# A routed mixture of experts on one core: chunks of 512 tokens instead of 256, gathers ahead of scatters that keep no order, one DMA for each expert's matrix

## The chip, the core and the metric

The kernel runs on one core of a Trainium2 chip. The core has a tensor engine (PE, whose weight loads the profile lists as PEld), a vector engine (DVE), a scalar engine (ACT), GpSimd (POOL) and a sync engine (SP) that issues DMAs. Each works through its own queue in order; they wait for one another by semaphores. [...] The metric is the device time of one execution in microseconds (us), as the median over runs.

## The reference

Three steps follow each other on an input of 8 x 3072 x 256: the real part of a two-dimensional Fourier transform, a gated network over all 24576 tokens, and a routed mixture of 8 experts. Only the last is touched by the change. With x the 24576 tokens of 256 numbers:

```python
logits = x @ w_gate                      # 24576 x 8
order = np.argsort(-logits.flatten())
# in this order a (token, expert) pair is taken if the token is still free
# and the expert has fewer than cap = 24576 // 8 = 3072 tokens
for e in range(8):
    mask = assigned == e                 # 3072 tokens
    h = np.maximum(x[mask] @ w1[e], 0.0) # 256 -> 1024
    out[mask] = h @ w2[e]                # 1024 -> 256
```

## The kernel before

The transform takes the span's first 315 us, the gated network runs to about 2016 us, the routed experts (class Moe2) fill the rest. All matrix products keep float32's precision by splitting each operand in a high and a low part (names ending in h and l) of type float32r and adding three products: high by high, high by low, low by high.

Moe2 works in eight rounds r, one expert closing in each; in round r PE computes that expert's 3072 tokens while the routing of the next expert runs beside it on DVE and ACT. The routing is a chain: a search over 32 bits for the threshold (one step per beat, with a tiny product cs, L1098 and L1100, between counts junk on DVE, L1113, and jka on ACT, L1116), then best (L1176), the ranks and the picks, which give idx, the token numbers of each slot. beat hands a share of this work to each of PE's steps, want forces it where a gather needs it.

A round has 12 chunks c of 256 tokens, a chunk has 4 steps g. What happens in a step is written out in run:

- plan holds the gathers (L1218, POOL: a DMA by index for 128 tokens, two for a chunk, into xg) and the loads of the next expert's weights (wload, L1227: w0r by two DMAs at step (10, 1), w1r by eight at step (10, 3)). wsplit makes w0h, w0l, w1h and w1l of them in quarters, at the steps of CFG['sp'].
- ffn1 is 12 matmuls with 256 moving columns (L1277 to L1279) into one PSUM tile; ACT makes hh of it (L1282), DVE hl (L1283).
- ffn2 of the step two back (lag 2) is 12 matmuls with 256 columns (L1297 to L1299). After a chunk's last, ACT copies the two accumulators to y (L1302) and POOL scatters each to out by the token numbers in tok (L1303).
- For the next chunk xsplit makes gh on ACT and gl on DVE at step 1 (L1254, L1255), and xprep turns them on PE at steps 2 and 3, four float32r transposes against identr each (L1265), with an ACT copy to xh or xl behind (L1266).

All scatters write the tensor out, so each waits until the one ahead has landed. Queues keep the order in which run writes the instructions; POOL's holds gathers, weight loads, scatters and the little copies tok.

The line that sets when gathers are asked for:

```python
at = (r, c - 2, 0) if c > 2 else (r - 1, *CFG[f'g{c}'])
```

with g0 = (10, 2), g1 = (10, 3), g2 = (12, 2), the last meaning step 2 of chunk 0.

Of the kernel before, what the change touches and what calls it, by code (L numbers as in the profile page):

```python
# [90 lines left out]
class Narrow:  # L91
    """weights of double precision as float32, in DRAM, a part at a time"""
# [20 lines left out]
    def clamp_one(self, i, t):  # L113
        """the magnitude's high word, within float32's exponents"""
# [18 lines left out]
    def once(self, src, dst, w, t):  # L133
        """a small part, into a tile"""
# [16 lines left out]
def fft_phase(tc, x, xm, c_odd, c_even, c_dim, c_alt, PQ_d, R_d, narrow=(), nxt=None):  # L151
    nc = tc.nc
# [13 lines left out]
    # rows 384 + 768 i of every batch  # L166
# [293 lines left out]
    # the first batch  # L460
# [47 lines left out]
    # the last batch, with the next phase's preparation beside it  # L508
# [27 lines left out]
def _token_ids():  # L536
    """true token of partition p in tile T = (block, half, sign)"""
    ids = np.zeros((128, 192), np.int32)
    p = np.arange(128)
    for blk in range(48):  # L540
        for sub in range(2):
# [4 lines left out]
            plus = np.where(cls == 1, k, S - k)      # U + V  # L546
            minus = np.where(cls == 1, S - k, k)     # U - V
# [6 lines left out]
def _lay_w(wg, wv):  # L554
    """by (gate or value, half): rows 0 to 127; an empty row and rows 255 down to 129. Row 128 by (matrix, f-tile)"""
# [5 lines left out]
class Moe1:  # L561
# [12 lines left out]
    def gv_load(self, c):  # L574
        """three f-tiles of the gate and value weights, rows 0 to 127 and 256 down to 129"""
# [27 lines left out]
    def task(self, k, arg):  # L603
        """the weights' preparation beside the end of the transform"""
# [30 lines left out]
    def small(self):  # L635
# [4 lines left out]
        # (-1)^l by partition: -1 + 2 * (sum of the identity's even columns)  # L640
# [11 lines left out]
    def open_keep(self, keep):  # L652
# [9 lines left out]
        # the table with the sigmoid, which has the other functions too  # L662
# [14 lines left out]
    def wo_load(self, c):  # L677
        """two f-tiles of the output weights"""
# [11 lines left out]
    def wo_turn(self, c):  # L690
        """two f-tiles of the output weights, turned, in two parts"""
# [12 lines left out]
    def wo_gate(self, c):  # L704
        """the output weights' product with the router's, to stand behind them"""
# [32 lines left out]
    def prep(self, raw, part, pool=None):  # L738
        """row 128's share of P, and the parts of P and Q"""
# [49 lines left out]
    def mini_load(self):  # L789
        """token 1536 of every batch, for which V is zero"""  # L790
# [71 lines left out]
    def hand_over(self):  # L862
        """the routing's start"""
# [11 lines left out]
    def run(self, LAG=4):  # L875
# [73 lines left out]
CFG = {'NV': 768, 'T': (1, 1, 1, 2, 1), 'cap': 0.2, 'f1': 2, 'f2': 2, 'g0': (10, 2), 'g1': (10, 3), 'g2': (12, 2),  # L949
# [6 lines left out]
def _route_consts():  # L956
# [5 lines left out]
    # slots; an expert's weights' rows, by its number from the end, with their multipliers; the numbers from the end  # L962
    slot = q[:, None] + 128 * np.arange(24)[None]
    wb = np.concatenate([q[:, None] + 128 * np.arange(2)[None] + 256 * NE,
                         q[:, None] + 128 * np.arange(8)[None] + 1024 * NE], 1)
    wm = np.array([-256] * 2 + [-1024] * 8)[None].repeat(128, 0)
# [5 lines left out]
class Moe2:  # L972
    def __init__(self, tc, w1, w2, out, c_mats, c_io, c_num, rounds=NE):
        self.tc, self.nc = tc, tc.nc
        self.w1 = w1.rearrange("e d f -> (e d) f")
        self.w2 = w2.rearrange("e f d -> (e f) d")
# [3 lines left out]
    def open_keep(self, keep, L, ident, X2_d):  # L980
        """what routing keeps, before the last of the logits"""
# [8 lines left out]
        self.num = keep.tile([128, 52], F32, name="num")  # L990
# [9 lines left out]
    def fill_keep(self):  # L1000
# [4 lines left out]
        self.slot, self.wb, self.wm, self.rio = num[:, 0:24], num[:, 24:34], num[:, 34:44], num[:, 44:52]  # L1005
# [5 lines left out]
    def grow(self, g, i):  # L1011
        """the first round's V for 16 tiles, in three steps"""
# [10 lines left out]
    def turn(self, p, c, n):  # L1023
        """n blocks of K's columns from block c on; the last tiles stand first"""
# [6 lines left out]
    def count0(self, i, c, n, junk):  # L1031
        """how many of some of K's columns are not negative"""
# [4 lines left out]
    def odd(self, kk):  # L1037
        """the columns from CFG['NV'] on with the last bit set in the order of floats, for the sign's sum"""
# [20 lines left out]
    def route(self, r):  # L1059
        """the expert that closes in round r: its number and its tokens' ranks"""  # L1060
# [75 lines left out]
        # ranks in the order (partition, tile): those above the threshold, then those at it  # L1136
# [4 lines left out]
        # the expert's weights' rows  # L1141
        wi = R.tile([128, 10], I32, name="wi", bufs=2)
# [28 lines left out]
    def best(self, out, V, lim, op):  # L1171
        """the greatest over the experts, each under its limit or with its penalty"""
# [5 lines left out]
    def pick(self, r):  # L1178
        """idx[r], slot by slot: pick the row of ranks that holds the slot, count the tiles before it"""
# [34 lines left out]
    def gather(self, r, c):  # L1214
        x = self.R.tile([128, 2, XW], F32, name="xg", bufs=CFG['xb'])
        for t in range(2):
            j = 2 * c + t
            self.nc.gpsimd.indirect_dma_start(  # L1218
                out=x[:, t], out_offset=None, in_=self.X2_d,
                in_offset=bass.IndirectOffsetOnAxis(ap=self.idx[r][:, j:j + 1], axis=0))  # L1220
        self.xg[r, c] = x
# [244 lines left out]
```

## Time and profile before

| | |
|---|---|
| median of 3 runs | 3421.25 us (3420.2 to 3422.5) |
| span of the profiled execution | 3409.2 us |
| around the span, against the median | 12.05 us |
| PE busy | 3192.7 us, 94% |
| DVE, POOL, ACT busy | 79%, 57%, 48% |
| mean granted clock of PE | 0.970 |

The span runs from the first to the last instruction. PE is "busy" while a matmul is in flight; matmuls overlap, so how fast they go is read from the distance of their starts. In a timeline a row gives the start, the length, the engine, the line of the kernel, the operation and its tiles; a bracket gives the idle time of the engine before it and who ended it. "issue" and "remote" are idle times for which the profile shows no releaser among the core's instructions.

### The profile page before, as it was taken

What the parts mean: (1) busy time and instruction counts of PE and PEld (TensorE: products, weight loads), DVE (VectorE), ACT (ScalarE), POOL (GpSimd) and SP (SyncE); (2) the same over time, 40 slices, a digit from 0 to 9 for tenths busy, and PEclk for the clock granted to TensorE, in tenths of its full rate; (3) what the DMA queues carried; (4) which work ended last, traced back from release to release, by engine and by line L of the source; (5) the groups of instructions that cost most, each with busy time, mean ns of one, the idle gap of its engine ahead of it and who ended that gap; (6) DMA issues with size and microseconds to landing.
All of it is one profiled execution on the core that took longest, in us unless ns stands there. A gap on an engine that the chain in (4) does not pass through costs nothing.

```text
span 3409.2 us, 68465 instructions
## 1 busy us (share of the span) xinstructions
PE 3192.7 (94%) x25857; PEld 3147.1 (92%) x25857; DVE 2700.6 (79%) x5727; ACT 1630.9 (48%) x3078; POOL 1944.9 (57%) x1933
## 2 busy tenths in 40 slices
PE   6787999999999999999999973999999999999998
PEld 5776999999999999999999963999999999998998
DVE  8998788888888888888888888777877777775332
ACT  3334344445444444444444444646465555553333
POOL 4656677777777777777777742343434343433432
PEclk8999999999999999999999986999999999999999
DMA  5547011111111111111111001121212121111211
GB/s 220 174 156 209 23 27 30 36 30 36 29 36 28 37 27 30 36 30 36 30 36 29 27 14 41 42 63 42 65 42 63 43 63 51 53 53 51 60 48 37
DMA packets 105016, 185.72 MB, mean 54 GB/s; under 512 B 15885, under 2 KB 80486, under 8 KB 101614
## 3 DMA queue, kind: packets, MB, share of 16 engines
q1 hardware_dynamic: 80430, 113.35, 11.5%
q0 software_dynamic: 23808, 67.92, 6.6%
q8 instruction: 204, 3.34, 0.4%
q14 instruction: 126, 1.03, 0.1%
q10 hardware_dynamic: 448, 0.07, 0.0%
HBM read 112.74 MB, written 68.53 MB: 53 GB/s over the span
## 4 chain that ended last, share of the span: by engine, by line
PE 84%; DVE 9%; issue 4%; DMA 1%; another core or an unknown queue 1%; ACT 1%; POOL 0%; SPq 0%; POOLq 0%; ACTq 0%; DVEq 0%
PE acc L786 8%; PE acc L785 8%; PE acc L787 8%; PE uv L760 8%; PE uv L761 8%; PE uv L762 8%; PE f L1277 6%; PE f L1297 6%; PE f L1279 5%; PE f L1278 5%; PE f L1299 5%; PE f L1298 5%; PE xt L1265 2%; DVE tm L1176 1%; PE rt L1204 1%
## 5 line engine op out<-in xcount | busy, mean ns | idle before, releaser
L906 POOL TENSOR_TENSOR h<-gt,z 128x512 f32<-128x512 f32 x575 | 748.1, 1301 | 437.3 <-ACT gt L921 437.3
L908 ACT CAST hh<-h 128x512 fp32r<-128x512 f32 x576 | 358.1, 622 | 746.6 <-POOL h L906 726.7
L760 PE MATMUL uv<-pqh,gh 128*128 128x256 f32 x2304 | 651.8, 283 | 9.1 <-DVE z L775 9.1
L786 PE MATMUL acc<-ol,hh 128*128 128x264 f32 x2304 | 656.3, 285 | 0.0
L785 PE MATMUL acc<-oh,hh 128*128 128x264 f32 x2304 | 655.6, 285 | 0.0
L787 PE MATMUL acc<-oh,hl 128*128 128x264 f32 x2304 | 655.4, 284 | 0.0
L761 PE MATMUL uv<-pql,gh 128*128 128x256 f32 x2304 | 653.0, 283 | 0.0
L762 PE MATMUL uv<-pqh,gl 128*128 128x256 f32 x2304 | 649.7, 282 | 0.0
L770 DVE SCALAR_TENSOR_TENSOR us<-bc,w,uv 128x256 f32<-128x256 f32 x1152 | 501.9, 477 | 159.4 <-PE uv L762 150.0
L1303 POOL DMA_INDIRECT out_dram<-y,tok x192 | 200.1, 1042 | 702.8 <-ACT y L1302 461.2
L1283 DVE SCALAR_TENSOR_TENSOR hl<-f,hh 128x512 fp32r<-128x512 f32 x384 | 265.0, 690 | 344.6 <-ACT hh L1282 323.1
L917 POOL TENSOR_TENSOR hl<-h,hh 128x320 fp32r<-128x320 f32 x574 | 507.0, 883 | 0.0
L1297 PE MATMUL f<-w1h,hh 128*128 128x256 f32 x1536 | 450.7, 293 | 9.5 <-ACT y L1302 7.5
L1277 PE MATMUL f<-xh,w0h 128*128 128x256 f32 x1536 | 452.8, 295 | 1.8 <-issue 1.8
L760 PEld LDWEIGHTS uv<-pqh,gh 128*128 128x128 f32 x2304 | 436.2, 189 | 10.2 <-issue 9.3
L1278 PE MATMUL f<-xl,w0h 128*128 128x256 f32 x1536 | 435.5, 284 | 2.4 <-issue 2.4
L762 PEld LDWEIGHTS uv<-pqh,gl 128*128 128x128 f32 x2304 | 437.4, 190 | 0.0
L1299 PE MATMUL f<-w1h,hl 128*128 128x256 f32 x1536 | 435.4, 283 | 1.3 <-issue 1.3
L1279 PE MATMUL f<-xh,w0l 128*128 128x256 f32 x1536 | 435.9, 284 | 0.6 <-issue 0.4
L1298 PE MATMUL f<-w1l,hh 128*128 128x256 f32 x1536 | 433.8, 282 | 2.0 <-issue 2.0
L761 PEld LDWEIGHTS uv<-pql,gh 128*128 128x128 f32 x2304 | 435.2, 189 | 0.0
L785 PEld LDWEIGHTS acc<-oh,hh 128*128 128x128 f32 x2304 | 435.2, 189 | 0.0
(440 smaller groups left out, 7692.9 us busy)
## 6 DMA issues: line engine op xcount, KB each, us to landing
X_d<-x SPq DMA_DIRECT2D x48, 528.0 KB
xt<-in_x_dram SPq DMA_DIRECT2D x24, 1024.0 KB
pq<-PQ_d SPq DMA_DIRECT2D x48, 256.0 KB
bc<-R_d SPq DMA_DIRECT2D x48, 256.0 KB
PQ_d<-po SPq DMA_DIRECT2D x24, 384.0 KB
dw<-in_wgv_dram SPq DMA_DIRECT2D x16, 384.0 KB
PQ_d<-po SPq DMA_DIRECT2D x8, 386.0 KB
dw<-in_moe_w_out_dram SPq DMA_DIRECT2D x8, 384.0 KB
```

The source lines that it names most:

```text
L760: pe.matmul(o, wh, h[:, q], start=True, stop=False)
L761: pe.matmul(o, wh, l[:, q], start=False, stop=False)
L762: pe.matmul(o, wl, h[:, q], start=False, stop=True)
L785: pe.matmul(o, x, wh, start=(ft == 0), stop=False)
L786: pe.matmul(o, x, wl, start=False, stop=False)
L787: pe.matmul(o, y, wh, start=False, stop=(ft == NF - 1))
L906: (g if n < N else v).tensor_mul(h[m], gt.pop(m), z.pop(m)[:, :, 1])
L1277: pe.matmul(p[:, i], wh[:, d, s], xh[:, d], start=(d == 0), stop=False)
L1278: pe.matmul(p[:, i], wh[:, d, s], xl[:, d], start=False, stop=False)
L1279: pe.matmul(p[:, i], wl[:, d, s], xh[:, d], start=False, stop=(d == 1))
L1297: pe.matmul(o, hh[:, i, s], wh[:, f], start=(f == 0), stop=False)
L1299: pe.matmul(o, hl[:, i, s], wh[:, f], start=False, stop=(f == 7))
```

## The change

All of it is in Moe2, but for docstrings and comments that go away and for the host's layout of the weights.

- A chunk is 512 tokens, six to a round; the steps are counted as before by (c, g) with c from 0 to 11, two c to a chunk. ffn1 of a step makes 128 hidden rows for 512 tokens: 6 matmuls with 512 columns. ffn2 is 12 matmuls with 256 columns as before, for four groups of 128 tokens; two accumulators share a PSUM bank, and y holds two of them.
- xsplit and xprep give way to xturn: four float32 transposes against ident straight from xg, ACT's copy xh, and DVE's subtraction xl from the same PSUM tile xt, of which there is one. The two halves of the next chunk's columns stand at steps 2 and 3 of the odd c.
- Gathers for c > 1 are planned at (r, c - 2 - c % 2, c % 2), the first two at steps 2 and 3 of (r - 1, 10).
- The scatters are put in a group without dependences among themselves ("rows").
- w1 and w2 are laid out on the host so that a partition's share of an expert's matrix is one row of 8 KB; wload is one DMA, wi one column.
- At the start, tiles 2 and 3 are picked and gathered before the first turn.

```diff
     def wload(self, r, k):
         w = self.R.tile([128, 2, F2] if k == 0 else [128, 8, D], F32, name=f"w{k}r")
-        src, n, o = (self.w1, 2, 0) if k == 0 else (self.w2, 8, 2)
-        for i in range(n):
-            self.nc.gpsimd.indirect_dma_start(
-                out=w[:, i], out_offset=None, in_=src,
-                in_offset=bass.IndirectOffsetOnAxis(ap=self.ew[r][:, o + i:o + i + 1], axis=0))
+        self.nc.gpsimd.indirect_dma_start(
+            out=w.rearrange("p i f -> p (i f)"), out_offset=None, in_=(self.w1, self.w2)[k],
+            in_offset=bass.IndirectOffsetOnAxis(ap=self.ew[r], axis=0))
...
+    def xturn(self, r, c, h):
+        nc, R, ps = self.nc, self.R, self.ps
+        x = self.xg[r, c]
+        if h == 0:
+            self.xt = R.tile([128, 2, 512], F32R, name="xh", bufs=2), R.tile([128, 2, 512], F32R, name="xl", bufs=2)
+            self.tok[r, c] = t = R.tile([128, 4, 1], I32, name="tok", bufs=3)
+            nc.gpsimd.tensor_copy(t, x[:, :, D:D + 1].bitcast(I32))
+        p = ps.tile([128, 512], F32, name="xt", bufs=CFG['xt'])
+        for t in range(4):
+            nc.tensor.transpose(p[:, t * 128:t * 128 + 128], x[:, t, h * 128:h * 128 + 128], self.ident)
+        xh, xl = self.xt
+        nc.scalar.copy(xh[:, h], p)
+        nc.vector.tensor_sub(xl[:, h], p, xh[:, h].bitcast(F32))
...
-        p = ps.tile([128, 2, 256], F32, name="f1", bufs=CFG["f1"])
-        for i in range(2):
-            s = slice(g * 256 + i * 128, g * 256 + i * 128 + 128)
-            for d in range(2):
-                pe.matmul(p[:, i], wh[:, d, s], xh[:, d], start=(d == 0), stop=False)
-                pe.matmul(p[:, i], wh[:, d, s], xl[:, d], start=False, stop=False)
-                pe.matmul(p[:, i], wl[:, d, s], xh[:, d], start=False, stop=(d == 1))
+        p = ps.tile([128, 512], F32, name="f1", bufs=CFG["f1"])
+        s = slice(f * 128, f * 128 + 128)
+        for d in range(2):
+            pe.matmul(p, wh[:, d, s], xh[:, d], start=(d == 0), stop=False)
+            pe.matmul(p, wh[:, d, s], xl[:, d], start=False, stop=False)
+            pe.matmul(p, wl[:, d, s], xh[:, d], start=False, stop=(d == 1))
...
+            if f == 7 and t % 2 == 1:
+                y = R.tile([128, 2, D], F32, name="y", bufs=3)
+                nc.scalar.copy(y, self.p2[t // 2])
+                for i in range(2):
+
+                    d = nc.gpsimd.indirect_dma_start(
+                        out=self.out, in_=y[:, i], in_offset=None,
+                        out_offset=bass.IndirectOffsetOnAxis(ap=self.tok[r, c][:, t - 1 + i], axis=0))
+                    self.tc.add_to_no_dep_group("rows", d.ins)
...
-                at = (r, c - 2, 0) if c > 2 else (r - 1, *CFG[f'g{c}'])
-                if at[1] == 12:
-                    at = (r, 0, at[2])
+                at = (r, c - 2 - c % 2, c % 2) if c > 1 else (r - 1, 10, 2 + c)
```

POOL's queue at the last change of expert stood so before (out_dram rows are scatters, xg rows gathers, xN how many follow in a row):

```order
L1303 DMA out_dram<-y,tok 24576x256 x2
L1227 DMA w0r<-in_moe_w_dram,wi 128x1024 x2
L1253 COPY tok<-xg 128x2
L1303 DMA out_dram<-y,tok 24576x256 x2
L1218 DMA xg<-X_d,idx 128x264 x4
L1227 DMA w1r<-in_moe_w_dram,wi 128x256 x8
L1253 COPY tok<-xg 128x2
```

and stands so now, with the end of the chunk ahead:

```order
L1293 DMA out_dram<-y,tok 24576x256 x4
L1250 COPY tok<-xg 128x4
L1225 DMA w0r<-in_moe_w_dram,wi 128x2048
L1293 DMA out_dram<-y,tok 24576x256 x4
L1219 DMA xg<-X_d,idx 128x264 x4
L1225 DMA w1r<-in_moe_w_dram,wi 128x2048
L1250 COPY tok<-xg 128x4
L1219 DMA xg<-X_d,idx 128x264 x4
```

Each weight load is a single issue, four scatters and four gathers stand together, and between changes of expert the three rows out_dram x4, tok, xg x4 repeat.

DVE's queue in the last round held one subtraction for a chunk's tokens, gl, of a chunk not yet turned:

```order
L1283 SCALAR_TENSOR_TENSOR hl<-f_44176,hh 128x512
L1255 TENSOR_TENSOR gl<-xg,gh 128x512
L1283 SCALAR_TENSOR_TENSOR hl<-f_44217,hh 128x512
L1283 SCALAR_TENSOR_TENSOR hl<-f_44256,hh 128x512
L1283 SCALAR_TENSOR_TENSOR hl<-f_44291,hh 128x512
```

and holds two for twice the tokens now, between the last steps of the chunk ahead:

```order
L1272 SCALAR_TENSOR_TENSOR hl<-f_39671,hh 128x512
L1256 TENSOR_TENSOR xl<-xt,xh 128x512
L1272 SCALAR_TENSOR_TENSOR hl<-f_39705,hh 128x512
L1256 TENSOR_TENSOR xl<-xt,xh 128x512
L1272 SCALAR_TENSOR_TENSOR hl<-f_39738,hh 128x512
```

The subtraction moved from ahead of the transposes to behind them.

## Rows read from the trace of the kernel before

**Rows 1.** The page: busy us and share of the span, by engine.
```profile
PE 3192.7 (94%) x25857; PEld 3147.1 (92%) x25857; DVE 2700.6 (79%) x5727; ACT 1630.9 (48%) x3078; POOL 1944.9 (57%) x1933
```

**Rows 2.** Steady window: length, PE busy (matmuls), granted clock, DMA share, GB/s.
```profile
2496.00:2530.00 34.00, 34.00 (x300) 1.00 0.13 41
```

**Rows 3.** Windows of equal length at the changes of expert; same columns.
```profile
2236.00:2270.00 34.00, 27.96 (x215) 0.90 0.31 90
...
3224.00:3258.00 34.00, 25.95 (x204) 0.85 0.21 63
sum 238.00, PE 197.83; mean PE 28.26
```

**Rows 4.** Timeline of PE, last round: start us, length us, instruction.
```profile
3250.33 0.28 PE L1279 MATMUL f<-xh,w0l 128*128 128x256 f32 x1
...
3250.93 0.28 PE L1298 MATMUL f<-w1l,hh 128*128 128x256 f32 x1
...
3252.24 0.28 PE L1277 MATMUL f<-xh,w0h 128*128 128x256 f32 x1
...
3255.10 0.28 PE L1277 MATMUL f<-xh,w0h 128*128 128x256 f32 x1
```

**Rows 5.** Timeline of PE in the transform, 384 columns.
```profile
109.84 0.34 PE L336 MATMUL xx<-odd,lo 128*128 128x384 f32 x1
...
113.48 0.34 PE L336 MATMUL xx<-odd,lo 128*128 128x384 f32 x1
```

**Rows 6.** Timeline of PE around a float32 group.
```profile
2115.14 0.28 PE L1299 MATMUL f<-w1h,hl 128*128 128x256 f32 x1
2115.26 0.60 PE L1028 MATMUL rt<-ident,V 128*128 128x128 f32 x4
...
2115.82 0.28 PE L1278 MATMUL f<-xl,w0h 128*128 128x256 f32 x1
```

**Rows 7.** Timeline at the first expert; bracket: idle time before, and its releaser.
```profile
2105.17 0.47 PE L1277 MATMUL f<-xh,w0h 128*128 128x256 f32 x1
...
2105.44 0.41 PE L1278 MATMUL f<-xl,w0h 128*128 128x256 f32 x1
...
2107.36 0.41 PE L1278 MATMUL f<-xl,w0h 128*128 128x256 f32 x1
...
2108.18 0.97 POOL L1218 DMA_INDIRECT xg<-X_d,idx  x1 [2.88 <-DVE idx L1210]
...
2112.73 0.62 ACT L1254 CAST gh<-xg 128x512 fp32r<-128x512 f32 x1 [0.60 <-DMA xg<-X_d,idx]
```

**Rows 8.** Timeline of ACT and DVE, a late step of the routing.
```profile
2553.28 4.35 DVE L1176 SCALAR_TENSOR_TENSOR tm<-V,t,tm 128x192 f32<-128x192 f32 x7
...
2557.06 0.60 ACT L1282 ACTIVATE hh<-f 128x512 fp32r<-128x512 f32 x1 [2.13 <-PE f L1279]
...
2558.13 0.68 DVE L1283 SCALAR_TENSOR_TENSOR hl<-f,hh 128x512 fp32r<-128x512 f32 x1
```

**Rows 9.** Timeline at the last change of expert, all engines.
```profile
3227.00 0.99 POOL L1303 DMA_INDIRECT out_dram<-y,tok  x1 [2.25 <-DMA out_dram<-y,tok]
...
3233.76 0.28 PE L1279 MATMUL f<-xh,w0l 128*128 128x256 f32 x1
...
3239.76 0.60 ACT L1282 ACTIVATE hh<-f 128x512 fp32r<-128x512 f32 x1 [6.90 <-remote]
...
3241.43 0.75 PE L1265 MATMUL xt<-identr,gh 128*128 128x128 f32 x4 [4.14 <-ACT w0h L1239]
...
3242.80 0.95 POOL L1227 DMA_INDIRECT w1r<-in_moe_w_dram,wi  x1 [0.30 <-issue]
```

**Rows 10.** PE in the first 11.3 us of seven chains, columns as above.
```profile
2898.40:2909.70 11.30, 9.31 (x77) 1.00 0.33 94
...
sum 79.10, PE 69.33; mean PE 9.90
```

**Rows 11.** PE beside seven chains of five issues, columns as above.
```profile
sum 50.40, PE 50.40; mean PE 7.20
```

More of the change, by code (lines that the diff above doesn't have):

```diff
@@ L963, in _route_consts @@
     slot = q[:, None] + 128 * np.arange(24)[None]
[L964 to L966 removed]
+    wb = q[:, None] + 128 * NE
+    wm = np.full((128, 1), -128)
     rio = (NE - np.arange(NE))[None].repeat(128, 0)
@@ L1243, in eng, with ffn1 @@
         return getattr(self.nc, n)
-    def xsplit(self, r, c):
-        nc, R = self.nc, self.R
+    def xturn(self, r, c, h):
+        nc, R, ps = self.nc, self.R, self.ps
         x = self.xg[r, c]
-        h = R.tile([128, 2, D], F32R, name="gh")
-        l = R.tile([128, 2, D], F32R, name="gl")
-        self.xs = h, l
-        self.tok[r, c] = t = R.tile([128, 2, 1], I32, name="tok", bufs=4)
-        nc.gpsimd.tensor_copy(t, x[:, :, D:D + 1].bitcast(I32))
-        nc.scalar.copy(h, x[:, :, 0:D])
-        self.eng(CFG['xsub']).tensor_sub(l, x[:, :, 0:D], h.bitcast(F32))
-    def xprep(self, k):
-        nc, R, ps = self.nc, self.R, self.ps
-        if k == 0:
-            self.xt = R.tile([128, 2, 256], F32R, name="xh", bufs=2), R.tile([128, 2, 256], F32R, name="xl", bufs=2)
-        p = ps.tile([128, 2, 256], F32R, name="xt", bufs=CFG['xt'])
-        for h in range(2):
-            for t in range(2):
-                nc.tensor.transpose(p[:, h, t * 128:t * 128 + 128], self.xs[k][:, t, h * 128:h * 128 + 128], self.identr)
-        nc.scalar.copy(self.xt[k], p)
+        if h == 0:
[8 more added lines that the diff above has]
+        nc.vector.tensor_sub(xl[:, h], p, xh[:, h].bitcast(F32))
         return self.xt
-    def ffn1(self, r, x, g):
+    def ffn1(self, r, x, f):
         nc, ps, R = self.nc, self.ps, self.R
@@ L1284, in ffn1, with ffn2 @@
         self.hid = hh, hl
-    def ffn2(self, r, c, g, hid):
+    def ffn2(self, r, c, f, hid):
         nc, ps, R = self.nc, self.ps, self.R
@@ L1289, in ffn2 @@
         (wh, wl), (hh, hl) = self.ws[r, 1], hid
-        for i in range(2):
-            f = 2 * g + i
-            for t in range(2):
-                if f == 0:
-                    self.p2[t] = ps.tile([128, 512], F32, name="f2", bufs=CFG['f2'])[:, 0:256]
-                o = self.p2[t]
-                s = slice(t * 128, t * 128 + 128)
-                pe.matmul(o, hh[:, i, s], wh[:, f], start=(f == 0), stop=False)
-                pe.matmul(o, hh[:, i, s], wl[:, f], start=False, stop=False)
-                pe.matmul(o, hl[:, i, s], wh[:, f], start=False, stop=(f == 7))
-                if f == 7:
-                    y = R.tile([128, D], F32, name="y", bufs=4)
-                    nc.scalar.copy(y, o)
-                    nc.gpsimd.indirect_dma_start(
-                        out=self.out, out_offset=bass.IndirectOffsetOnAxis(ap=self.tok[r, c][:, t], axis=0),
-                        in_=y, in_offset=None)
+        for t in range(4):
+            if f == 0 and t % 2 == 0:
+                self.p2[t // 2] = ps.tile([128, 2, 256], F32, name="f2", bufs=2)
+            o = self.p2[t // 2][:, t % 2]
+            s = slice(t * 128, t * 128 + 128)
+            pe.matmul(o, hh[:, s], wh[:, f], start=(f == 0 and t % 2 == 0), stop=False)
+            pe.matmul(o, hh[:, s], wl[:, f], start=False, stop=False)
+            pe.matmul(o, hl[:, s], wh[:, f], start=False, stop=(f == 7 and t % 2 == 1))
+            if f == 7 and t % 2 == 1:
[6 more added lines that the diff above has]
+                    self.tc.add_to_no_dep_group("rows", d.ins)
     def chain(self):
@@ L1353, in run @@
             self.advance(0)
-        self.xsplit(0, 0)
-        for i in range(2):
-            x = self.xprep(i)
         for i in range(CFG['pre2']):
@@ L1360, in run @@
         self.gather(0, 1)
+        for h in range(2):
+            x = self.xturn(0, 0, h)
         late = []
@@ L1437, in _laid @@
     wgv, w128 = _lay_w(inputs["moe_w_gate"], inputs["moe_w_val"])
-    rest = [(n, inputs[n]) for n in ("moe_w_out", "moe2_w_gate", "moe2_w1", "moe2_w2")]
+    w1, w2 = (w.reshape(NE, n, 128, -1).transpose(0, 2, 1, 3).reshape(NE * 128, -1)
+              for w, n in ((inputs["moe2_w1"], D // 128), (inputs["moe2_w2"], F2 // 128)))
+    rest = [("moe_w_out", inputs["moe_w_out"]), ("moe2_w_gate", inputs["moe2_w_gate"]), ("moe2_w1", w1), ("moe2_w2", w2)]
     given = []
```

42 lines of the change are left out of this document (20 added, 22 removed), and 3 rows, old and new, of the table CFG.

## The prediction

> **What bounds the kernel now.** I read the busy line first: the tensor engine (PE) is at work for 94% of the span [rows 1], so a gain must come off its path or out of its holes. The windows come next, because the change touches only the routed experts (2016 to 3409 us). In a steady stretch PE is busy 34.00 of 34 us at the full clock [rows 2]; there only fewer or cheaper matmuls help. At each of the seven changes of expert a window of the same length has 28.26 us of PE work on average, at granted clocks of 0.85 to 0.95 [rows 3]. That is 34 - 28.26 = 5.7 us idle; the seven clocks average 0.90, so about a fifth of 34 us ran at half clock and lost half of itself, 3.3 us. About 9 us per change, 63 us in all: that is the only other large thing to win.
>
> The profiled span is 3409.2 us and the median of the runs 3421.25; I let the same 12.05 us lie around the new span, and add and subtract against the median.
>
> **First products, 512 columns instead of 256.** 4608 matmuls become 2304. From 3252.24 to 3255.10 stand 24 of 256 columns in 2.86 us, 119.2 ns each [rows 4]. No row has 512 columns. The nearest is 384: 21 in 3.64 us from 109.84 to 113.48, 173.3 ns [rows 5]. The line through both adds 54.1 ns per 128 columns, so 512 would take 227.4 ns, against 2 x 119.2 = 238.4. The saving is 11.0 ns x 2304 = 25 us. One end is proportional cost: nothing. [...]
>
> [...]
>
> **Turning the tokens.** Before, each 256 tokens have two groups of four float32r transposes. From the matmul ahead of a group (3250.33) to the second one behind it (3250.93) pass 0.60 us, where two steps of 119.2 ns would be 0.239: a group costs 0.36 us [rows 4]. After, each 512 tokens have two groups of four float32 transposes against ident, the form that the routing uses on V: from 2115.14 to 2115.82 is 0.68 us, so 0.44 a group [rows 6]. Per 512 tokens 4 x 0.364 = 1.456 becomes 2 x 0.439 = 0.878, and 48 x 0.578 = 27.7 us go. This is PE's own time in the stretch where PE is never idle, so it counts in full. The two scalar copies gh and one pair of xh, xl copies per chunk go too, and y is copied in two pieces instead of four; ACT is at 48% [rows 1], so that is worth nothing by itself.
>
> **Start of the first expert.** The first product now needs four gathered tiles and not two. Before, it starts at 2105.17, and tiles 2 and 3 are only asked for at 2108.18 and land at 2112.73 [rows 7]. Behind that landing come two turns with a copy like hh's 0.60 and a subtraction like hl's 0.68 [rows 8]; gl's subtraction and seven weight DMAs no longer stand ahead. I place the first product at about 2115.5, 10 us late. [...] Net 7.5 us lost, bounds 4 and 10.
>
> **VectorE's late parts.** The second half of a turn now waits for xl of the first half (xt has one buffer), and the next chunk's first product waits for xl of the second half; behind such a wait stands everything of PE. Behind the last ffn1 step come 0.44 of transposes, ACT's hh and xh of 0.60 each and 0.68 for xl, 2.32 us; PE has the transposes, 12 matmuls of ffn2 (1.43 us) and four products (0.91) to do, 2.78 us. So 0.46 us are to spare. The spare is gone where DVE sits in a long block: hh is there at 2557.06 + 0.60 = 2557.66, but seven L1176 operations hold DVE from 2553.28 for 4.35 us and hl starts only at 2558.13 and ends 1.15 us behind hh [rows 8]. Seven rounds have such a place, with blocks at other steps too; the bounds are 0 and 7 x 4.35 = 30 us, and I take 1.9 a round, 13 us, nearer to the 1.15.
>
> **POOL's queue at a change of expert.** The chain from 3227.00 is 13 DMA issues without a pause: one scatter, four gathers, eight w1r [rows 9]. Within it the other engines stop being released by PE: the last product of a step starts at 3233.76, yet ACT's hh, which needs only that and a buffer long free, starts at 3239.76 after 6.90 us of "remote" idle, with DVE all but idle; and PE then waits 4.14 us [rows 9]. In the first 11.3 us of the seven chains PE has 9.90 us of work, so 1.40 are lost there on average and 1.99 in the worst chain [rows 10]; the other 9 - 1.4 = 7.6 us come later in the chain and behind it. After, w1r is one issue: four scatters, four gathers, one w1r, nine issues, some 11.5 us. The tail of the chain goes. I take 4 of the 7.6 us, as DVE still has best and V to do there: 7 x 4 = 28 us gained; bounds 0 and 53.
>
> **POOL's queue in each chunk.** This is the price of unordered scatters and early gathers. Before, a scatter waits for the landing of the one ahead (2.25 us [rows 9]), so three issues at most follow each other in a steady stretch. After, four scatters, a copy of tok and four gathers follow at once: eight issues, 8 x 1.27 = 10.2 us, in some 40 chunks away from the changes of expert. (tok waits for gathers that landed long before; the gathers behind it are needed a chunk later, so their own delay costs nothing.) The rows give both ends. Seven chains of five issues (one scatter, four gathers) cost PE nothing: 50.40 us busy of 50.40 [rows 11]. The first 11.3 us of the long chains cost 1.40 [rows 10]. Eight lie between; half of these are scatters, and no weights are among them. I take 0.4 us x 40 = 16 us lost; bounds 0 and 40 x 1.99 = 80.
>
> **The end.** Before, the last scatter waits for the landing of the one ahead like the others; after, four scatters stand some 1.3 us apart and end at about the same time: nothing.
>
> **Sum.** -25 - 27.7 + 7.5 + 13 - 28 + 16 = -44, so 3421.25 - 44 = 3377 us. What I cost at nothing has cover: gathers are asked for a chunk of PE work (some 23 us) ahead. Where a gather has no such cover, as at the start, it takes 2112.73 - 2108.18 = 4.6 us from issue to use [rows 7]; that is the price for each place where the cover fails.
>
> **Rivals.** (1) Chains of eight hold PE as the long ones do. For it: same engine, same pace of issue, and the first hole in the long chains falls inside their first 11.3 us [rows 10]. Against: five issues cost nothing [rows 11]. At 1.4 us each it is 56 in place of 16: 3417, no change. At 1.99 it is 80: 3441, slower. It decides against the change from (44 + 16) / 40 = 1.5 us per chain on. (2) The stalls at the changes of expert have nothing to do with the length of the chain and stay: 28 us less gained, 3405. For it: nothing in the trace ties them to one queue; against: hh's wait lies within the w1r issues [rows 9]. (3) 512 columns cost twice 256, and that edit does nothing: 3402. Against: the 384 row. [...] (5) The change of expert is freed wholly: 25 us more, 3352.
>
> **How the numbers follow.** Forecast 0.50, 3377, with its own range of 3358 to 3396. Rival 1 has 0.18 (0.05 for no change, 0.11 slower, the rest just faster); rival 2 has 0.11, rival 3 0.11, rivals 4 and 5 together 0.10. About 0.2%, 7 us, is what a measurement of this kernel can tell from no change. Faster: 0.50 + 0.02 + 0.11 + 0.11 + 0.10 = 0.84, less 0.04 where rivals 2 or 3 meet a mild form of rival 1, which gives no change or worse: 0.80. No change 0.05 + 0.02 = 0.07, slower 0.11 + 0.02 = 0.13. The range of 3347 to 3428 takes in rivals 2, 3 and 5, nearly all of 4 and the milder half of 1.
>
> **What would show it.** [...] The first product near 2115.5. In windows of 34 us at the changes of expert some 32 us of PE work. In steady stretches PE below 34.00 by about 0.4 us a chunk, the holes lying 8 to 11 us behind the first of four scatters, ACT's hh late there; 1.5 us or more there would make the prediction wrong, and so would holes at each turn with PE waiting for xl, or a first product later than 2118.

## The result and the profile after

The changed kernel takes 3368.48 us (median of 4 runs, 3366.52 to 3369.51) where the kernel before took 3421.88 (3420.2 to 3423.49) on the same chip: ratio 0.9847, 95% interval 0.9833 to 0.9861, or 53.4 us less. The forecast was 3377 in a range of 3347 to 3428.

The profiled execution of after has a span of 3366.6 us and a time of 3368.34, so 1.7 us lie around a span. The trace of before (3409.2) thus belongs to an execution some 10 us shorter than the median of its runs, and the 12.05 us that the prediction laid around the span are mostly that. Between the two traces lie 42.6 us; why the medians lie 10 us further apart, no trace shows. By place the 42.6 us are (acc names the network's last products, L785 to L787; 0.4 us stand ahead of the first):

| stretch, us | before | after | change | forecast |
|---|---|---|---|---|
| gated network, first to last acc | 1688.8 | 1667.0 | -21.8 | 0 |
| last acc to the first product of the experts | 89.4 | 98.5 | +9.1 | +7.5 net |
| first to last product of the experts | 1294.6 | 1256.4 | -38.2 | -52 |
| last product to the end | 9.4 | 18.1 | +8.7 | 0 |

The page of after, busy us by engine; against [rows 1] PE has 59 us less:

```profile
PE 3133.5 (93%) x23169; PEld 2974.8 (88%) x23169; DVE 2712.7 (81%) x5727; ACT 1524.2 (45%) x2790; POOL 1853.0 (55%) x1821
```

PE in after, the last products of a step with 512 columns and the first of ffn2 (start us, length us, instruction), which answers to [rows 4]:

```profile
2619.94 0.40 PE L1266 MATMUL f<-xh,w0h 128*128 128x512 f32 x1
2620.18 0.39 PE L1267 MATMUL f<-xl,w0h 128*128 128x512 f32 x1
2620.40 0.39 PE L1268 MATMUL f<-xh,w0l 128*128 128x512 f32 x1
2620.63 0.28 PE L1285 MATMUL f<-w1h,hh 128*128 128x256 f32 x1
```

Three steps in 0.69 us, 230 ns each; over the whole trace the mean is 231.

The windows at the changes of expert (length, PE busy with the number of matmuls, granted clock as a share of the full one, DMA share, GB/s), which answer to [rows 3]:

```profile
2216.00:2250.00 34.00, 27.66 (x155) 0.90 0.31 102
2380.00:2414.00 34.00, 28.06 (x161) 0.89 0.32 104
...
sum 238.00, PE 202.03; mean PE 28.86
```

28.86 us of work in 34, where there were 28.26 and the forecast said 32: the stall at the change of expert seems untouched. But it is another stall. POOL in after at the second change (the bracket: idle before, and its releaser), against [rows 9]:

```profile
2386.84 0.99 POOL L1293 DMA_INDIRECT out_dram<-y,tok  x1 [7.57 <-issue]
2389.54 0.97 POOL L1293 DMA_INDIRECT out_dram<-y,tok  x1 [1.70 <-DMA out_dram<-y,tok]
2392.71 0.97 POOL L1293 DMA_INDIRECT out_dram<-y,tok  x1 [2.20 <-DMA out_dram<-y,tok]
2395.39 1.26 POOL L1293 DMA_INDIRECT out_dram<-y,tok  x1 [1.71 <-DVE tm L1173]
2396.96 0.99 POOL L1219 DMA_INDIRECT xg<-X_d,idx  x1 [0.30 <-issue]
2398.26 1.31 POOL L1219 DMA_INDIRECT xg<-X_d,idx  x1 [0.30 <-issue]
2399.87 1.95 POOL L1219 DMA_INDIRECT xg<-X_d,idx  x1 [0.30 <-issue]
2402.13 2.56 POOL L1219 DMA_INDIRECT xg<-X_d,idx  x1 [0.30 <-issue]
```

The scatters are still ordered, against what the title and the list of the change say: each starts some 2.7 or 3.2 us behind the last, and the second and third are put down to that one's landing (the fourth, at the same distance, to DVE's tm). The change calls add_to_no_dep_group alone; in a run below (a_nodep), which calls declare_no_dep too and has a memset between them, 1.3 us stand between two scatters. So four scatters hold the queue for 10 us, and the next expert's gathers stand behind them. PE, at the same place, takes its transposes one by one as the gathers land:

```profile
2399.84 0.33 PE L1253 MATMUL xt<-ident,xg 128*128 128x128 f32 x1
2401.45 0.33 PE L1253 MATMUL xt<-ident,xg 128*128 128x128 f32 x1 [1.29 <-DMA xg<-X_d,idx]
2403.69 0.33 PE L1253 MATMUL xt<-ident,xg 128*128 128x128 f32 x1 [1.91 <-DMA xg<-X_d,idx]
2406.54 0.48 PE L1253 MATMUL xt<-ident,xg 128*128 128x128 f32 x1 [2.52 <-DMA xg<-X_d,idx]
```

PE's waits in after behind the start, from 2110 us on (waiter, releaser: us in all, times, longest):

```profile
PE xt L1253 <- DMA xg<-X_d,idx: 31.7, 21, 2.6
PE xt L1253 <- DVE xl L1256: 10.1, 7, 1.9
PE f L1267 <- DVE xl L1256: 3.7, 6, 2.4
```

And the end, POOL in after; the last product starts at 3348.51:

```profile
3349.48 0.97 POOL L1293 DMA_INDIRECT out_dram<-y,tok  x1 [9.95 <-ACT y L1290]
...
3358.02 0.97 POOL L1293 DMA_INDIRECT out_dram<-y,tok  x1 [1.70 <-DMA out_dram<-y,tok]
```

These are the first and the last of four, 8.5 us apart. Before, two stood there 3.2 us apart, so the order of the scatters makes 5.4 of the 8.7 us. The other 3.4 come behind the last scatter: from its start to the end of the span pass 8.5 us and not 5.1. That is so in every trace with one issue per expert matrix, those made from the kernel before too (b_w1, b_w1_2, b_w1n), and in no other. Why, no run tells.

Three questions were left. Why is a network shorter whose code was not touched? What do the scatters' order and the queue's order cost? And were the holes before really made by the chain of issues? The runs came in six groups, each on one chip, and that turned out to matter. B to F are five different chips; which one A was is not on record. No chip was used at two times, so "chip" below may also stand for something else that stayed the same within a group:

| chip | kernel before | kernel | us | ratio to before, 95% interval |
|---|---|---|---|---|
| A | 3421.9 | the changed kernel | 3368.5 | 0.9847, 0.9833 to 0.9861 |
| B | 3416.1 | b_num64 | 3408.3 | 0.9976, 0.9966 to 0.9985 |
| B | | a_num64 | 3379.1 | 0.9893, 0.9878 to 0.9908 |
| B | | a_exp64 | 3355.9 | 0.9825, 0.9811 to 0.9838 |
| B | | a_nodep | 3370.0 | 0.9861, 0.9846 to 0.9876 |
| C | 3353.8 | a_same | 3351.9 | 0.9993, 0.9984 to 1.0002 |
| C | | b_w1 | 3356.7 | 1.0004, 0.9995 to 1.0013 |
| C | | a_256 | 3369.6 | 1.0051, 1.0037 to 1.0064 |
| C | | a_gfirst | 3320.6 | 0.9901, 0.9886 to 0.9916 |
| D | 3353.3 | b_same | 3352.7 | 0.9997, 0.9988 to 1.0007 |
| D | | b_w1_2 | 3355.2 | 1.0006, 0.9996 to 1.0016 |
| E | 3422.6 | b_w1n | 3346.6 | 0.9778, 0.9765 to 0.9792 |
| F | 3352.3 | a_gfirst_2 | 3320.3 | 0.9905, 0.9888 to 0.9921 |

### The profile page after: what moved, and what is told of

It is laid out like the page before. It is cut to its first block, busy times and chain, and to the rows that moved or that the text cites. A ratio compares the mean times of both kernels' runs of the same rounds, so it can differ in the third digit from the quotient of the medians.

```text
span 3366.6 us, 62238 instructions
## 1 busy us (share of the span) xinstructions
PE 3133.5 (93%) x23169; PEld 2974.8 (88%) x23169; DVE 2712.7 (81%) x5727; ACT 1524.2 (45%) x2790; POOL 1853.0 (55%) x1821
## 4 chain that ended last, share of the span: by engine, by line
PE 83%; DVE 9%; issue 4%; DMA 2%; ACT 1%; POOL 1%; SPq 0%; POOLq 0%; DVEq 0%; ACTq 0%
PE acc L785 8%; PE acc L786 8%; PE acc L787 8%; PE uv L760 8%; PE uv L761 8%; PE uv L762 8%; PE f L1266 5%; PE f L1287 5%; PE f L1285 5%; PE f L1286 5%; PE f L1267 5%; PE f L1268 5%; DVE tm L1173 1%; PE xt L1253 1%; PE xx L336 1%
## 5 line engine op out<-in xcount | busy, mean ns | idle before, releaser
L785 PE MATMUL acc<-oh,hh 128*128 128x264 f32 x2304 | 655.9, 285 | 0.0
L760 PE MATMUL uv<-pqh,gh 128*128 128x256 f32 x2304 | 646.3, 281 | 9.5 <-DVE z L775 9.5
L787 PE MATMUL acc<-oh,hl 128*128 128x264 f32 x2304 | 654.5, 284 | 0.0
L761 PE MATMUL uv<-pql,gh 128*128 128x256 f32 x2304 | 645.5, 280 | 0.0
L762 PE MATMUL uv<-pqh,gl 128*128 128x256 f32 x2304 | 645.0, 280 | 0.0
L760 PEld LDWEIGHTS uv<-pqh,gh 128*128 128x128 f32 x2304 | 434.9, 189 | 10.5 <-issue 8.5
L1285 PE MATMUL f<-w1h,hh 128*128 128x256 f32 x1536 | 443.1, 288 | 0.0
L762 PEld LDWEIGHTS uv<-pqh,gl 128*128 128x128 f32 x2304 | 435.1, 189 | 0.0
L786 PEld LDWEIGHTS acc<-ol,hh 128*128 128x128 f32 x2304 | 435.0, 189 | 0.0
L787 PEld LDWEIGHTS acc<-oh,hl 128*128 128x128 f32 x2304 | 434.4, 189 | 0.0
L785 PEld LDWEIGHTS acc<-oh,hh 128*128 128x128 f32 x2304 | 434.1, 188 | 0.0
L774 DVE TENSOR_TENSOR z<-us,uv 128x512 f32<-128x512 f32 x576 | 395.4, 687 | 19.8
```

Source lines behind the costliest of these rows:

```text
L760: pe.matmul(o, wh, h[:, q], start=True, stop=False)
L761: pe.matmul(o, wh, l[:, q], start=False, stop=False)
L762: pe.matmul(o, wl, h[:, q], start=False, stop=True)
L785: pe.matmul(o, x, wh, start=(ft == 0), stop=False)
L786: pe.matmul(o, x, wl, start=False, stop=False)
L787: pe.matmul(o, y, wh, start=False, stop=(ft == NF - 1))
```

## Experiments

**The place of the network's tiles.** The one thing in the change that reaches the network is the size of num, a small table that is allocated ahead of it: 34 columns and not 52, so every tile of the network lies 64 bytes lower. Two kernels put the tiles elsewhere and change nothing else (ones, padded too, moves the experts' tiles by 64 bytes more):

```diff
 a_num64 (from the changed kernel)
-        self.num = keep.tile([128, 34], F32, name="num")
+        self.num = keep.tile([128, 50], F32, name="num")[:, 0:34]
-        self.ones = R.tile([128, NT], F32, name="ones")
+        self.ones = R.tile([128, NT + 16], F32, name="ones")[:, 0:NT]
 b_num64 (from the kernel before)
-        self.num = keep.tile([128, 52], F32, name="num")
+        self.num = keep.tile([128, 68], F32, name="num")[:, 0:52]
 (ones as above)
```

> The changed kernel, doing the same work, with num made longer so that the gated network's tiles lie where the kernel before has them; the experts' tiles move by 128 bytes. Theory P: the gated network goes back to 1688 us and 119.6 ns, the time is about 3390. Rival: 3368, the gated network stays at 1667.

> The kernel before, doing the same work, with the tile num made 64 bytes longer, so that every tile of the gated network (315 to 2016 us) lies where it lies in the changed kernel (modulo 128 bytes); the routed experts' tiles move by 128 bytes. Theory P (the address of the moving operand sets the pace): the products of L760 to L762 go from 119.6 to 116.8 ns from start to start, the gated network takes 1667 instead of 1688 us, the time is about 3400. Rival (the 22 us that the gated network lost in the changed kernel's trace are a matter of the execution or the chip): 3422 and 119.6 ns.

The first and last acc of the network, in after and then in a_num64 (duration ns min/median/max, first and last start us):

```profile
L785 PE MATMUL acc<-oh,hh x2304: 278/283/422, 326.6 to 1993.3; 128*128 128x264 f32 x192
```

```profile
L785 PE MATMUL acc<-oh,hh x2304: 278/283/422, 327.3 to 2016.1; 128*128 128x264 f32 x192
```

With the tiles put back, the changed kernel's network takes 1688.8 us and not 1666.7 between these starts, as much as in the kernel before. The times agree: a_num64 takes 3379.1 us, a_exp64 below, which differs from it in the line of num alone, 3355.9 on the same chip. The gap between starts of the 256-column products (L760 to L762) goes with it: 116.8 to 117.0 ns on average in after, 119.2 to 120.5 in a_num64. So the 22 us are a matter of address alone. What rule decides it is open: 64 bytes further up (b_num64) the network takes 1683.1 us, neither the one nor the other, and the expectation for it (1667 us, 3400 in all) missed: 3408.3.

**The experts' tiles.** The same, tried on the experts alone: the line of ones above, without that of num.

> The changed kernel, doing the same work, with the tiles of the routed experts alone 64 bytes further, so that xh, xl, w1h and w1l, which lie 64 bytes past a multiple of 128, start at one. Theory P: products of the experts get 1 to 3 ns cheaper for 256 columns (117.5 to about 115.5) and up to 3 for 512, 7000 products, 10 to 15 us: about 3355. Rival (address without effect): 3368.

The paces of the experts' matmuls stayed (231 ns of 512 columns, 118 of 256), and from first to last product it takes 1243.9 us, a_num64 on the same chip 1245.6. The idea falls, though its number, 3355, came out. That is luck: the lower time next to that of chip A belongs to the chip: taking the network's 22 us off a_num64 gives 3357 for the changed kernel on chip B.

**512 columns or 256.**

```diff
-        for d in range(2):
-            pe.matmul(p, wh[:, d, s], xh[:, d], start=(d == 0), stop=False)
+        for n in range(2):
+            m = slice(n * 256, n * 256 + 256)
+            for d in range(2):
+                pe.matmul(p[:, m], wh[:, d, s], xh[:, d, m], start=(d == 0), stop=False)
...
```

> The changed kernel with its first products taken back to 256 columns, twelve matmuls per step and not six (float32 turning, gathers, scatters and weights as changed). By the paces read in the two traces, 231 ns of 512 columns against 2 x 119.2, 7.4 ns x 2304 = 17 us are given back; by the prediction's 227.4, 25 us; by the rival that 512 columns cost twice 256, nothing. Ratio to the changed kernel 1.005, 1.0075 or 1.000.

3369.6 against a_same's 3351.9: 17.7 us, the number worked out from the paces. 512 columns pay, by two thirds of what the forecast said.

**Scatters truly unordered.** The scatters are declared free of order, with a short memset between them:

```diff
+                    nc.gpsimd.memset(self.gap, 0.0)
...
+                    self.tc.declare_no_dep(d.ins, group="rows", reason="each row of out is written once")
```

> [...] Scatters then stand 1.3 to 1.6 us apart instead of 2.7 to 3.2. Theory Q (at a change of expert the turn waits for gathers that stand in POOL's queue behind four scatters in order): PE's wait for xg goes from 50 us to 15 to 25, the time to 3340 to 3350. Rival R (chains of eight or nine issues hold back what PE releases, as in the long chains of the kernel before): 0.4 to 2 us lost in each of 48 chunks, 3370 to 3440.

It is slower than the ordered one would be on that chip (3370 against 3357). This is the state that the prediction had costed: 24 chains of eight issues and 7 of nine. POOL in a_nodep, the first and last scatter of a chain and its last gather:

```profile
2318.37 1.00 POOL L1294 DMA_INDIRECT out_dram<-y,tok  x1 [18.11 <-ACT y L1291]
...
2322.23 0.97 POOL L1294 DMA_INDIRECT out_dram<-y,tok  x1 [0.19 <-issue]
...
2327.39 0.95 POOL L1220 DMA_INDIRECT xg<-X_d,idx  x1 [0.30 <-issue]
```

PE's waits in a_num64, and then in a_nodep, both on chip B, from 2010 us on:

```profile
PE cs L1095 <- DVE junk L1110: 49.4, 31, 2.4
PE xt L1253 <- DMA xg<-X_d,idx: 44.9, 25, 12.5
PE xt L1253 <- DVE xl L1256: 10.7, 6, 1.9
```

```profile
PE cs L1096 <- DVE junk L1111: 75.8, 62, 2.4
PE xt L1254 <- DVE xl L1257: 31.1, 13, 4.6
PE xt L1254 <- DMA xg<-X_d,idx: 18.5, 4, 13.0
```

The wait for gathered tiles at the changes goes, and waits for DVE come in their place: behind the start 32.6 of the 75.8 us for the counts of the routing's search, where a_num64 has none. From first to last product PE is idle for 1264.30 - 1195.50 = 68.8 us in a_nodep and 41.3 in a_num64.

What a chain costs can be read chunk by chunk, from first product to first product. The 18 chunks that hold a chain of eight while the search runs take 1.4 to 2.5 us more than the same chunks of a_num64, 2.0 on average. The six such chunks of the last two rounds, where no search runs any more, take 2 us more in all. The chunks at the changes of expert, with their nine issues, take 19 us less in all. So a late release costs PE something where the search stands behind it. That is rival 1, which put 1.4 to 1.99 on a chain, on a chip of this kind. On the other kind (below) it was not tried.

**Gathers ahead of the scatters at the change of expert.** The four scatters of the step (10, 1) are held back, and issued behind the gathers and w1r:

```diff
-                for i in range(2):
-                    d = nc.gpsimd.indirect_dma_start(...)
-                    self.tc.add_to_no_dep_group("rows", d.ins)
+                self.held.append((r, c, t, y))
+                if not (c == 4 and r + 1 < self.rounds):
+                    self.scatter()
...
+                    if (c, g) == (10, 3):
+                        self.scatter()
```

> The changed kernel itself, once more, so that the next two can be held against it on one chip. By the ratio of its first runs, 0.985, some 3365 to 3370 us where the kernel before takes 3416 to 3421. If the ratio is not within 0.983 to 0.987, the comparison of different chips misled.

> The changed kernel with one move: at the seven changes of expert the four scatters of the step are issued behind the next expert's four gathers and its w1r, not ahead of them. Theory: the scatters, each of which waits for the landing of the one ahead, hold the gathers back by some 10 us, PE's wait for gathered tiles (50.4 us in all, 13.2 of it at the start) falls to about 15, and 25 to 35 us go: ratio to the changed kernel 0.990 to 0.993. Rival: what comes next is as late (the weights' DMA, VectorE's work for V, or PE's releases late behind nine issues), another wait takes its place, and the time stays within 5 us.

a_same came out at the time of the kernel before (ratio 0.9993), so the comparison of different chips had misled, as its text puts it. a_gfirst takes 31.3 us less than a_same on the same chip (3320.6 against 3351.9). POOL at the second change in a_gfirst:

```profile
2382.36 0.96 POOL L1219 DMA_INDIRECT xg<-X_d,idx  x1 [7.90 <-DVE tm L1163]
2383.63 0.95 POOL L1219 DMA_INDIRECT xg<-X_d,idx  x1 [0.30 <-issue]
...
2386.13 1.06 POOL L1219 DMA_INDIRECT xg<-X_d,idx  x1 [0.30 <-issue]
2387.50 0.94 POOL L1225 DMA_INDIRECT w1r<-in_moe_w_dram,wi  x1 [0.30 <-issue]
2388.74 1.00 POOL L1298 DMA_INDIRECT out_dram<-y,tok  x1 [0.30 <-ACT w0h L1237]
2393.97 1.56 POOL L1298 DMA_INDIRECT out_dram<-y,tok  x1 [4.23 <-DMA out_dram<-y,tok]
```

PE's waits from 2110 us on, in a_same and then in a_gfirst:

```profile
PE xt L1253 <- DMA xg<-X_d,idx: 26.6, 22, 2.6
PE xt L1253 <- DVE xl L1256: 9.5, 5, 1.9
```

```profile
PE xt L1253 <- DVE xl L1256: 21.5, 10, 2.4
```

The account closes from first to last product: 26.6 us of waits for gathers gone, 12.0 more for xl, and the clock. The traces' clock records have the granted shares 1.0 and 0.5; from 2110 us on the clock was at half for 44.4 us in a_same and for 3.4 in a_gfirst. Half of the difference, 20.5 us, is won back: -26.6 + 12.0 - 20.5 = -35.1, measured 1240.7 to 1205.6. (PE's busy time in the stretch, which holds the same matmuls, fell by 20.0 us.) The wait's price nearly doubled through the clock that fell behind it.

> The changed kernel with the scatters behind the gathers at the changes of expert, once more, for another chip. Theory: the wait for gathered tiles at the changes belongs to the order of POOL's queue and not to the chip, so the 31 us less come on any chip: some 3321 us (ratio 0.990) where the kernel before takes 3353, and 3335 to 3340 (ratio 0.975 to 0.977) where it takes 3416 to 3422, since the nine issues that now follow each other (w0r, four gathers, w1r, the first scatters) may make PE's releases late there. Rival: on such a chip that lateness takes all of it, and it takes 3360 or more, ratio 0.983.

3320.3 on a chip where the kernel before takes 3352.3, the same again. It beats both kernels; on a chip of the kind of A, B and E it has not been run, so how much of it holds there is open.

**One issue per expert matrix, alone.** The kernel before with w0r and w1r by one issue each (the host lays the weights out for it):

```diff
-        src, n, o = (self.w1, 2, 0) if k == 0 else (self.w2, 8, 2)
-        for i in range(n):
-            self.nc.gpsimd.indirect_dma_start(
-                out=w[:, i], out_offset=None, in_=src,
-                in_offset=bass.IndirectOffsetOnAxis(ap=self.ew[r][:, o + i:o + i + 1], axis=0))
+        self.nc.gpsimd.indirect_dma_start(
+            out=w.rearrange("p i f -> p (i f)"), out_offset=None, in_=(self.w1, self.w2)[k],
+            in_offset=bass.IndirectOffsetOnAxis(ap=self.ew[r][:, 0:1], axis=0))
```

> The kernel before with one part of the change alone: an expert's w1r and w2r come with one DMA issue each, from a layout that the host makes, and not with eight and two (the first products', the turning's, the gathers' and the scatters' code and the size of num stay). Theory of the prediction: the length of the issue chain makes the stalls at the seven changes of expert; 4 of 7.6 us of each go, 28 us, up to 53: ratio 0.992 to 0.985, and the windows of 34 us at the changes show 31 to 32 us of PE work and not 28.3. Rival: the stalls have another cause (the gathers of the next expert land late, VectorE's work on best and V), and nothing goes: ratio 1.000, 28.3 us.

No effect: the rival's number. Of the 2.9 us that it takes more, within the interval of no change, the end of the span would explain 3.4 (see above). But on this chip the kernel before takes 68 us less than on A, and it left no trace there. The next pair, on another chip, gave one:

> The kernel before itself, for a trace on the chip where the next run stands. So far it took 3422 and 3416 us on two chips and 3354 on a third, where no trace of it was taken. Theory: the chips differ in the stalls at the seven changes of expert alone (57 us of PE's holes and slow clock), so a trace with a time near 3354 has no holes in the chains of 13 issues and its stretch from first to last product of the experts is some 1237 us; one near 3416 has holes as in [rows 3], and 1295 us. Rival: the chips differ everywhere (matmul pace, network), and the holes are there at either time.

> The kernel before with one issue per expert matrix once more, beside a trace of the kernel before on the same chip. Theory: without the chain of 13 issues nothing holds PE at the changes, on any chip: 3354 to 3360 us, so ratio 0.981 to 0.983 where the kernel before takes 3416 and 1.000 where it takes 3354. Rival: on a chip where the kernel before takes 3416 this one takes 3390 or more.

b_same takes the 1237 us of its theory between first and last product. b_w1_2 with 3355.2 is where its theory puts it too, but on a chip with nothing to win, so it tests nothing.

The kernel before from first to last product on chip A, and b_same on chip D (length, PE busy, clock, DMA share, GB/s):

```profile
2105.20:3399.80 1294.60, 1249.23 (x10632) 0.98 0.17 52
```

```profile
2104.40:3341.90 1237.50, 1228.13 (x10634) 1.00 0.18 54
```

The network takes the same on both (1688.8 and 1686.6 us); the 57 us lie in the experts alone, and there at the changes. The seven windows of 34 us at the changes, in b_same:

```profile
sum 238.00, PE 238.00; mean PE 34.00
```

No hole at all. POOL issues the same 13 DMAs in a row as in [rows 9], at the same pace; POOL's first two and the last of them, and ACT within them:

```profile
3179.70 0.99 POOL L1303 DMA_INDIRECT out_dram<-y,tok  x1 [2.24 <-DMA out_dram<-y,tok]
3180.99 1.01 POOL L1218 DMA_INDIRECT xg<-X_d,idx  x1 [0.30 <-issue]
...
3195.43 0.95 POOL L1227 DMA_INDIRECT w1r<-in_moe_w_dram,wi  x1 [0.30 <-issue]
```

```profile
3183.93 0.60 ACT L1282 ACTIVATE hh<-f 128x512 fp32r<-128x512 f32 x1 [2.13 <-PE f L1279]
...
3186.79 0.60 ACT L1282 ACTIVATE hh<-f 128x512 fp32r<-128x512 f32 x1 [1.23 <-PE f L1279]
...
3189.64 0.60 ACT L1282 ACTIVATE hh<-f 128x512 fp32r<-128x512 f32 x1 [0.68 <-PE f L1279]
```

hh starts every 2.86 us; PE's last product ahead of the second starts at 3186.47, 0.32 us earlier. In [rows 9] the same hh came 6.0 us behind its product. So a long chain does not hold PE's releases by itself: on some chips it does, on others not at all. Counted over the traces from 2115 us on, hh starts over 1 us later than its product and ACT's work ahead of it allow 14 times in before (up to 5.7 us), 14 times in b_num64, 9 times in b_w1n and 28 times in a_nodep, and not once in the seven traces from chips C, D and F. It does so in none of the three with the changed kernel's ordered scatters on A and B (after, a_num64, a_exp64) either. What sets these chips apart no run here tells.

**One issue per matrix, on a chip of the first kind.** b_w1, and num cut to 34 columns as in the changed kernel:

```diff
-        self.num = keep.tile([128, 52], F32, name="num")
+        self.num = keep.tile([128, 34], F32, name="num")
```

> The kernel before with one issue per expert matrix, and with num 34 columns wide as in the changed kernel, so that the gated network's tiles lie 64 bytes lower, as there. The network's code is that of before. Theory of the placement: first to last acc 1667 us and not 1689, 22 us less on any chip. Theory of the chain: without the 13 issues in a row no PE release is late on any chip, and the experts take 1237 us from first to last product. Together some 3334 us: ratio 0.994 where the kernel before takes 3353, 0.976 where it takes 3416 to 3422. Rivals: acc to acc stays 1689 (the shorter network belongs to something else in the changed kernel); on a chip where the kernel before takes 3416 the holes stay and it takes 3390.

This run fell on chip E, where the kernel before takes 3422.6: 76.0 us less, and 22 below what the changed kernel takes on A. The first and last acc, then PE from first to last product, then the sum of the seven windows of 34 us at the changes:

```profile
L785 PE MATMUL acc<-oh,hh x2304: 278/283/422, 327.8 to 1997.1; 128*128 128x264 f32 x192
```

```profile
2085.40:3332.00 1246.60, 1233.10 (x10633) 1.00 0.17 54
...
sum 238.00, PE 234.25; mean PE 33.46
```

Both causes are there in one run, with the matmuls of the kernel before: the network takes 1669.3 us by the place of its tiles, and the windows hold 33.46 us and not 28.26. From first to last product it takes 1246.6 us, not the 1237 of its theory, and 3346.6 in all where 0.976 times 3422.6 is 3340: its claim that no release is late on any chip failed. Releases are still late on this chip in the six issues that are left. PE's last product of a step, and ACT's hh that waits for it:

```profile
2389.30 0.28 PE L1275 MATMUL f<-xh,w0l 128*128 128x256 f32 x1
```

```profile
2393.37 0.60 ACT L1278 ACTIVATE hh<-f 128x512 fp32r<-128x512 f32 x1 [5.89 <-PE f L1275]
```

hh starts 4.1 us behind its product, 1.4 us after the chain's last issue ends at 2391.95. But PE has other work until then and loses 0.7 us at this place (0.19 at 2393.34, and 0.54 at 2394.74 for the hl of this hh). So shortening the row of 13 issues to six took nine tenths of the holes away on such a chip. The issues' number and the length of the rows that they fetch (8 KB for 4 and 1 KB) changed together, and no run parts the two.

## Why the prediction was right, and where it was not

The time came out 8 us below the forecast, inside the forecast's own range, and two of the larger terms held. The sum as a whole did not: errors of both signs cancelled, and that the time fits so well is luck. Without the network's 22 us, which no term foresaw, it would have been 3390, 13 us above the forecast and still inside its range.

- **First products.** Forecast 25 us from a line through 256 and 384 columns (227.4 ns); the paces give 231 ns and 17 us, a_256 gave 17.7. The term was mis-sized by a third. With that rival 3 (512 columns cost twice 256) falls. More than 25 us from this edit, for which rival 4 has its chance and a part of the range, no run shows: the runs showed 17 and 17.7.
- **Turning the tokens.** Forecast 0.44 us a group, two per 512 tokens. The median of 94 groups is 0.788 us from the matmul ahead to the second behind, less 0.230 and 0.118 for two steps: 0.44. Right, some 27.5 us; this and the start are read from the trace, and no run has them alone.
- **Start.** Forecast 10 us late and 7.5 net; it is 9.1 late. The 2.5 us between the two forecasts no run shows; by the clock records PE is at half the clock for 4.4 us from the first product on in before and for 2.2 in after, and half of the difference is 1.1 us.
- **VectorE's late parts.** Forecast 13; the waits for xl are 13.8 us.
- **Change of expert, -28.** This step failed: "four scatters, four gathers, one w1r, nine issues, some 11.5 us" took the scatters to follow each other at once. They wait for landings, take 10 us ahead of the gathers, and the cover that the prediction counted on ("gathers are asked for a chunk of PE work (some 23 us) ahead") fails at just these places. It had named the price of that, 4.6 us for each; seven times 4.6 is 32, and the wait is 31.7. The wait is made otherwise than that, by three transposes at each change that wait for the next gather, so the agreement is in part luck. The old stall went as forecast, or more (b_w1n: all but a tenth of it by the windows, and no release over 1 us late in after), and a new one took its place, with PE at half the clock for 51.2 us from 2110 us to the last product by the trace's clock records (47.8 before).
- **Chains of eight, +16.** Never formed, by the same error: the step "four scatters, a copy of tok and four gathers follow at once" took the name in the diff for the thing. The holes that it expected in steady stretches are all but absent: four windows of 34 us in after hold 33.65 to 33.91 us of PE work. Where chains of eight do form (a_nodep) they cost 2.0 us each beside the search, above the 1.5 from which rival 1 was to decide, and next to nothing beside no search; with what the gathers and the end win back, a_nodep is 13 us slower than the ordered scatters on its chip.
- **The end, nothing.** Failed: 8.7 us, of which 5.4 once more by the order of the scatters.
- **The network, untouched.** No term at all, since no line of it changed; 21.8 us.
- **Rivals 2 and 5.** Rival 2 had the stall independent of the chain: wrong on chips of the first kind (b_w1n), and on those of the second there is no stall. Rival 5, the stall freed wholly, is what b_w1n shows but for the new wait.

So the gain of 53 us on chip A is not what it looks like. PE's own work in the experts fell by some 44 us (17 and 27.5), and the late start, the waits for gathers and xl, the clock behind them and the end took more than that: from the last acc to the end the changed kernel on chip C takes 1357 us, the kernel before on chip D 1336. Up to the last acc it is 20 us ahead in these two traces, nearly all of it the network's, and on chip C the ratio is 0.9993. On chip A the gain is the old stall, which costs the kernel before some 57 us there by the difference to chip D, less the 16 us that the changed kernel takes longer between first and last product on A than on C (1256.4 against 1240.7; a_num64 on B 1245.6). Of these 16, 5.1 are longer waits for gathers and 3.4 the longer time at half the clock; the rest is open.

## What to carry to other kernels

Look at what an instruction waits for in the built program, not at what a call is named: here four ordered scatters held all that stood behind them in POOL's queue for 10 us, so the transfers that somebody waits for go first (a_gfirst, 31.3 us less). A hole in PE's work had a second price here, the granted clock behind it: 20.5 us beside 26.6 us of waits, four fifths as much as the hole. And repeat a small gain on a second chip and with the tiles in another place before it is put down to the edit: here the same two kernels differ by 53 us on one chip and by 2 on another.

## What was not expected of the hardware

- **Chips differ in one thing.** In three groups of runs (A, B, E) the kernel before takes 3416 to 3423 us, in three (C, D, F) 3352 to 3354. Its traces on A and D have the network within 2 us of each other, the same pace of issue and the same matmul paces (L760 to L762 119.2 to 120.5 ns). What differs is that within a row of POOL's DMA issues what waits for PE is released up to 6 us behind its product on the former, and 0.3 us behind it on the latter.
- **The address of tiles moves a matmul's pace.** 64 bytes of shift change the average step of a 256-column float32r product from 119.2 or more to 117.0 ns or less, and a stretch of 1689 us by 22, in both kernels and on several chips (first to last acc: 1667.0 to 1669.6 us in the lower place, 1686.6 to 1690.6 in that of before).
